# Float32 products for V, w_in split only for the last tile, and halves of 512 and 384 tokens in the second MLP

## The chip, the cores and the metric

The kernel runs on one core of a Trainium2 chip. The metric is the device time of one execution in microseconds (us), the median of several runs.

## The reference

Attention between 512 tokens and 32 state rows per head (8 batches, 8 heads of 64), in both directions, gives 544 rows of 512 features for each batch. Two MLPs follow (512 to 2048 to 512), each without a bias:

```python
a  = softmax(x @ state.T / 8);  xread = a @ state      # per batch and head
a2 = softmax(state @ x.T / 8);  sread = a2 @ x
t = concat([xread, sread])      # 4352 tokens x 512
h = t @ moe_w_in;  g = where(h >= 1, h, where(h <= -1, 0, (h + 1)**2 / 4))
t = g @ moe_w_out
h = t @ moe2_w_in;  g = max(h, 0) + alpha * min(h, 0)
out = g @ moe2_w_out
```

The weights reach the kernel as 8-byte floats, the rest of the work is done in float32.

## The kernel before, in words

**Precision.** A float32 operand can go to the matmul as it is, or it is split into a high part (a cast to float32r on ScalarE, `hi_`, line 72) and the rest (a subtraction on VectorE, `lo_`, line 75). A product of two split operands is three matmuls, hi x hi, hi x lo and lo x hi (`mm3`, line 78). The 8-byte weights are decoded by one ScalarE instruction (`dec0`) and four on VectorE (`dec1`).

**First MLP.** For the 4096 token rows of the eight batches the kernel does not form xread. It uses x_read @ w_in = a @ (state @ w_in): V = state @ w_in of a batch has 256 rows (8 heads x 32 state rows) and 2048 columns, and the hidden h is a product of the softmax weights with V (`h_mm`, line 545, tile hA). w_in is cut into four blocks of 512 columns (blk) and each into four tiles of 128 rows (c); a tile of 128 rows serves two heads. The step list (line 535) is 9 tiles of tokens (8 batches and a last tile with the 256 rows of sread) x 16 pieces of the hidden dimension. At step i the kernel issues the side work that was put at i with `at`, the products of step i + 2 into hA, the activation, the split of g of step i + 1, and the products with w_out into accA (`out_mm`, line 587). Batch 0 uses float32 products with w_out there, later ones split ones.

**V.** V of batch 0 is made by `vdirect` (line 431, tile vdp) from the split w_in and the split, block-diagonal state. V of batches 1 to 3 comes from one group of state rows, g = 0, in `vg_dir` (line 485, tile vgp): a head has 64 rows of w_in, so its matmuls use 64 of the 128 partitions, and the two heads of a tile of w_in are issued in turn into two PSUM buffers. V of batches 4 to 7 (g = 1) is made in batches 2 and 3, one head at a step, by `vg_mm` (line 496): the high and low parts of the head's 64 rows are read back from DRAM (wd) one under the other as ws, by a DMA on POOL's queue that casts (`vg_load`, line 469), and two matmuls over 128 partitions follow. ScalarE copies each result out of PSUM (vgo, line 476) and SP stores it to vd in DRAM, from where each batch loads and splits its part (vr, vw). The last tile has no V; it needs w_in itself, split, which it loads from wd (`w1s_load`, line 528).

**Around it.** PSUM has four buffers for hA, vdp, vgp and the attention's tiles (pool pp), and four for accumulators (pool pa). SBUF tiles come from two pools, 72 of 2 KB and 14 of 4 KB per partition. Most loads and stores are issued from SP in one queue; a store there waits for what it stores, and what stands behind it waits too. The attention of the next batch runs beside each batch. The order on each engine is the program's unless the compiling framework moves an instruction that is ready earlier.

**Second MLP.** Both products are done by a seven-product scheme on 2 x 2 blocks (`second`, line 929). The tokens are taken in five groups; each is two halves side by side, whose width HALF (line 37) is the column count of its matmuls. A group has 336 matmuls for the hidden layer (hB, line 771) and 336 for the output (accB, line 846), whatever the width; all weights (112 tiles of 256 KB) are loaded again for each group. Group 3 and group 4 change places in the token order (line 710).

Of the kernel before, what the change touches and what calls it, by code (L numbers as in the profile page):

```python
# [9 lines left out]
F32 = mybir.dt.float32  # L10
# [23 lines left out]
NF, NO = FF // 128, DM // 128  # L34
ROWS = S + NS
TOK = NB * ROWS
HALF = [448, 448, 448, 416, 416]


@with_exitstack  # L40
def kernel_body(ctx: ExitStack, tc: tile.TileContext, x, state, w1i, w1o, w2i, w2o, alpha, out):
# [12 lines left out]
    def V(name, dt=F32):  # L54
        return vp.tile([128, 1024], dt, tag="v", name=name)
# [4 lines left out]
    def PS(name):  # L60
        return pp.tile([128, 512], F32, tag="ps", name=name)
# [16 lines left out]
    def mm3(ps, terms):  # L78

        n = 3 * len(terms)  # L80
        k = 0
        for sh, sl, mh, ml in terms:
            for a, b in ((sh, mh), (sh, ml), (sl, mh)):
                pe.matmul(ps, a, b, start=(k == 0), stop=(k == n - 1))  # L84
                k += 1
# [5 lines left out]
    st1 = cp.tile([128, 256], F32, name="st1")  # L91


    vd = [[dp.tile([NH, 128, 512], F32, name=f"vd{g}_{k}") for k in range(4)] for g in range(2)]
    xd = dp.tile([NO, 128, TOK], F32, name="xd")
    w1d = dp.tile([8, 7, 128, 512], F32, name="w1d")
    w2d = dp.tile([8, 7, 128, 512], F32, name="w2d")
    wd = [dp.tile([2, DM, 512], F32, name=f"wd{k}") for k in range(4)]
    GRP = [1, 4]
    NR = 2  # L100

# [265 lines left out]
    def dec1(key):  # L367
        t = G.pop(("raw", key))
        r = G["dec", key]
        ri = r.bitcast(I32)  # L370
        words = t.bitcast(I32).rearrange("p (n t) -> p n t", t=2)
        lo_w, hi_w = words[:, :, 0], words[:, :, 1]
        dve.tensor_scalar(out=r, in0=r, scalar1=2.0 ** -15, scalar2=122876.0, op0=ALU.max, op1=ALU.min)
        yield
        dve.tensor_scalar(out=ri, in0=ri, scalar1=3, scalar2=0x3FFFFFFF,
                          op0=ALU.logical_shift_left, op1=ALU.bitwise_and)
        yield
        dve.scalar_tensor_tensor(out=ri, in0=lo_w, scalar=29, in1=ri,
                                 op0=ALU.logical_shift_right, op1=ALU.bitwise_or)
        yield  # L380
        dve.scalar_tensor_tensor(out=ri, in0=hi_w, scalar=-0x40000000, in1=ri,  # L381
                                 op0=ALU.bitwise_and, op1=ALU.bitwise_or)
        yield
        if key[0] == "wi":
            dec_hi(key)

    def dec_hi(key):
        name = "w_" + "_".join(map(str, key))
        h = U(name + "h", F32R)
        hi_(h, G["dec", key])  # L390
        W[key] = (h, U(name + "l", F32R))
# [5 lines left out]
    def decode(key, o):  # L397
        at(o - 1, dec0, key)
        at(o, dec1, key)
        if key[0] == "wi":  # L400
            at(o + 1, dec2, key)

    def split(t, name):
        h, l = U(name + "h", F32R), U(name + "l", F32R)
        hi_(h, t)
        lo_(l, t, h)
        return h, l

    def z_build(b):
        z = U(f"z{b}")  # L410
        pool.memset(z, 0.0)
        zz = z.rearrange("p (q r h d) -> p q r h d", q=2, r=2, h=2)
        sv = st1[:, b * 128:(b + 1) * 128].rearrange("p (q d) -> p q d", q=2)
        for k in range(4):
            p = slice(32 * k, 32 * k + 32)
            dve.tensor_copy(zz[p, :, k // 2, k % 2, :], sv[p])
        ps = PS(f"zt{b}")
        for k in range(4):
            pe.transpose(ps[:, k * 128:(k + 1) * 128], z[:, k * 128:(k + 1) * 128], ident)
        G["zf"] = U(f"zf{b}")  # L420
        act.copy(G["zf"], ps)
        G["z", b] = split(ps, f"zs{b}")

    def wi_load(blk, c):
        d_load(("wi", blk, c), w1i[c * 128:(c + 1) * 128, blk * 512:(blk + 1) * 512])

    def wi_store(blk, c):
        for k, t in enumerate(W["wi", blk, c]):
            ld.dma_start(out=wd[blk][k, c * 128:(c + 1) * 128, :], in_=t.bitcast(F32))

    def vdirect(b, blk):
        zh, zl = G["z", b]
        for q in range(2):
            ps = PS(f"vdp{b}{blk}{q}")
            mm3(ps, [(zh[:, c * 128:(c + 1) * 128], zl[:, c * 128:(c + 1) * 128], *W["wi", blk, c])
                     for c in (2 * q, 2 * q + 1)])
            h, l = U(f"vw{b}{blk}{q}h", F32R), U(f"vw{b}{blk}{q}l", F32R)
            hi_(h, ps)
            yield
            yield  # L440
            lo_(l, ps, h)
            VW[b, blk, q] = (h, l)

    def ld_stg(g):

        t = V(f"stg{g}")
        tv = t.rearrange("p (h u d) -> p h u d", h=NH, u=2)
        if g == 0:  # L450
            pool.memset(t, 0.0)
        for i in range(4):
            for u in range(2):
                hs = slice(u, NH, 2) if g == 0 else slice(0, NH)
                ld.dma_start(out=tv[32 * i:32 * i + 32, hs, u, :],
                             in_=state[GRP[g] + i, hs].rearrange("h n d -> n h d"))
        G["stg", g] = t

    def st_build(g, hh):
        t = G["stg", g]  # L460
        ps = PS(f"stp{g}{hh}")
        for k in range(4):
            c = (hh * 4 + k) * 128
            pe.transpose(ps[:, k * 128:(k + 1) * 128], t[:, c:c + 128], ident)
        ST[g, hh] = split(ps, f"sts{g}{hh}")
        if hh:
            del G["stg", g]

    def vg_load(g, blk, h):
        t = U(f"ws{g}{blk}{h}", F32R)  # L470
        pool.dma_start(out=t, in_=wd[blk][:, h * D:(h + 1) * D, :])
        G["w", g, blk, h] = t

    def vg_out(g, blk, h, ps):
        o = U(f"vgo{g}{blk}{h}")
        act.copy(o, ps)  # L476
        if g:
            G["vgo", blk, h] = o
        else:
            ld.dma_start(out=vd[g][blk][h], in_=o)  # L480

    def vg_store(blk, h):
        ld.dma_start(out=vd[1][blk][h], in_=G.pop(("vgo", blk, h)))

    def vg_dir(blk, c):
        wh, wl = W["wi", blk, c]
        ps = [PS(f"vgp0{blk}{2 * c + u}") for u in range(2)]
        for n in range(3):
            for u in range(2):
                h, rows = 2 * c + u, slice(64 * u, 64 * u + 64)  # L490
                k = slice((h % 4) * 128, (h % 4) * 128 + 128)
                pe.matmul(ps[u], ST[0, h // 4][n == 2][rows, k], (wh, wl, wh)[n][rows], start=(n == 0), stop=(n == 2))  # L492
        for u in range(2):
            vg_out(0, blk, 2 * c + u, ps[u])

    def vg_mm(g, blk, h):
        ws = G.pop(("w", g, blk, h))
        sh, sl = ST[g, h // 4]
        c = (h % 4) * 128
        ps = PS(f"vgp{g}{blk}{h}")  # L500
        pe.matmul(ps, sh[:, c:c + 128], ws, start=True, stop=False)
        pe.matmul(ps, sl[:, c:c + 128], ws, start=False, stop=True)  # L502
        vg_out(g, blk, h, ps)

    def vr_load(b, blk, q):
        g = 0 if b < 5 else 1
        i = b - GRP[g]
        t = U(f"vr{b}{blk}{q}")
        ld.dma_start(out=t, in_=vd[g][blk][4 * q:4 * q + 4, 32 * i:32 * i + 32, :])
        G["v", b, blk, q] = t  # L510
# [15 lines left out]
        return w2o[f * 128:(f + 1) * 128, :]  # L526

    def w1s_load(blk, c):
        h, l = U(f"w1s{blk}{c}h", F32R), U(f"w1s{blk}{c}l", F32R)
        for k, t in enumerate((h, l)):  # L530
            ld.dma_start(out=t.bitcast(F32), in_=wd[blk][k, c * 128:(c + 1) * 128, :])
        W["w1s", blk, c] = (h, l)


    steps = [(t, f) for t in range(NB + 1) for f in range(NF)]
# [453 lines left out]
    def at(i, fn, *a):  # L989
        side[i].append((fn, *a))  # L990
# [46 lines left out]
                at(o + 1, vr_lo, b, blk, q)  # L1037


    def vg_plan(g, start, per):  # L1040
        n = 0
        for blk in range(4):
            for h in range(NH):
                o = start + int(n * per)
                at(o - 2, vg_load, g, blk, h)
                at(o + 1, vg_mm, g, blk, h)
                at(o + 2, vg_store, blk, h)
                n += 1
        at(start - 2, ld_stg, g)
        at(start, st_build, g, 0)  # L1050
        at(start, st_build, g, 1)

    at(-2, ld_stg, 0)
    at(0, st_build, 0, 0)
    at(0, st_build, 0, 1)
    for blk in range(4):
        for c in range(4):
            at(max(1 + c, 4 * blk - 5 + c), vg_dir, blk, c)
    vg_plan(1, gi(2, 0), 1.0)

    for blk in (1, 2, 3):
        for c in range(4):
# [14 lines left out]
        at(gi(7, c + 3), xs_lo, c)  # L1077
    for blk in range(4):
        for c in range(4):
            at(gi(8, 4 * blk - 9 + c), w1s_load, blk, c)  # L1080

    def w2_plan(key, o):
        at(o - 3, d_load, key, src_w2p(*key[1:]) if key[0] == "w2i" else src_w2o(key[1]))
# [42 lines left out]
    scores(1)  # L1126
    run((dec1, ("wi", 0, 0)))
    dec0(("wi", 0, 1))
    run((first_max, 0), (first_max, 1), (dec2, ("wi", 0, 0)))
    run((first_turn, 0), (first_turn, 1), (dec1, ("wi", 0, 1)))  # L1130
    dec0(("wi", 0, 2))
    dec0(("wi", 0, 3))
    run((s6, 0, 0), (s6, 0, 1))
    dec2(("wi", 0, 1))
    run((dec1, ("wi", 0, 2)), (dec1, ("wi", 0, 3)))
    s7(0, 0)
    first_back(0)
    s7(0, 1)
    first_back(1)
    dec2(("wi", 0, 2))  # L1140
    dec2(("wi", 0, 3))
    dec0(("w1o", 0))
    run((s8, 0, 0), (s8, 0, 1), (vdirect, 0, 0))
    run((s9, 0, 0), (s9, 0, 1), (dec1, ("w1o", 0)))
# [44 lines left out]
```

## Time and profile before

| | |
|---|---|
| median of 3 runs | 1404.79 us (1403.83 to 1408.65) |
| the profiled execution | 1402.33 us, span 1400.3 us |
| first MLP, first matmul with w_out to the last hidden product of the last tile | 39.8 to 717.7 us |
| second MLP, from its first matmul | 717.7 to 1400.3 us |
| bytes moved | 312.30 MB, 223 GB/s |

The span is that of the instructions of the profiled execution; the time of a run has some 2 us around it. Engines work side by side, so a share of busy time says little of what an operation costs; that depends on which engine is waited for in the stretch in which it stands.

### The profile page before, as it was taken

The page shows a single profiled execution, that of the slowest core. Times are in us where ns is not written, and L with a number is a line of the kernel's source. Part 1 is how long each engine was busy: PE and PEld are TensorE (multiplying, and loading weights), DVE is VectorE, ACT ScalarE, POOL GpSimd, SP SyncE. Part 2 cuts the span into 40 slices and gives each one's busy share as a digit, 9 for nine tenths or more (in the row PEclk, how much of TensorE's full clock was granted, in tenths as well). Part 3 has the DMA queues.
Part 4 walks back from the last instruction along what each step waited for, and adds up shares of the span by engine and source line. Part 5 has one row for each costly group of instructions (what it writes and reads, how often), then busy time and mean ns, then how long its engine had stood idle before and what let it go on. Part 6 is the DMA issues. An engine that isn't in the chain of part 4 may idle for free.

```text
span 1400.3 us, 20902 instructions
## 1 busy us (share of the span) xinstructions
PE 1362.7 (97%) x6932; PEld 1169.8 (84%) x6932; DVE 1046.4 (75%) x1872; ACT 793.3 (57%) x1526; POOL 104.8 (7%) x123
## 2 busy tenths in 40 slices
PE   6899999999999999999999999999999999999998
PEld 4455688877788888887998999899999999999997
DVE  6877686767779787976669785778687868786873
ACT  4566676666677666775555453455454535454552
POOL 1000001231221111211101000000000000000000
PEclk9899999999999999999999999999999999999999
DMA  6897636589985665557777776777777687779774
GB/s 202 303 321 271 140 72 154 131 218 259 230 253 157 174 186 163 167 189 243 268 231 274 245 256 210 237 251 249 230 238 264 212 255 244 253 254 314 223 231 150
DMA packets 295964, 312.30 MB, mean 223 GB/s; under 512 B 144049, under 2 KB 179889, under 8 KB 295857
## 3 DMA queue, kind: packets, MB, share of 16 engines
q1 hardware_dynamic: 255504, 293.09, 66.1%
q0 software_dynamic: 33280, 8.51, 3.4%
q10 hardware_dynamic: 7072, 9.37, 1.9%
q8 instruction: 55, 0.90, 0.3%
q14 instruction: 53, 0.43, 0.1%
HBM read 237.90 MB, written 72.35 MB: 222 GB/s over the span
## 4 chain that ended last, share of the span: by engine, by line
PE 88%; DMA 5%; DVE 3%; ACT 2%; issue 1%; POOL 0%; SPq 0%; POOLq 0%; DVEq 0%; ACTq 0%
PE accB L846 24%; PE hB L771 23%; PE accA L605 20%; PE hA L84 12%; PE accA L597 4%; DMA vd<-vgo 2%; PE vgp L492 1%; PE sc L84 1%; PE vdp L84 1%; DMA ws<-wd 1%; DMA xr<-xd 1%; DMA xd<-oA 1%; PE sr L254 1%; DMA vr<-vd 0%; PE et L205 0%
## 5 line engine op out<-in xcount | busy, mean ns | idle before, releaser
L846 PE MATMUL accB<-gs,wv 128*128 128x448 f32 (+1 forms) x1680 | 336.2, 360 | 0.5 <-ACT o L864 0.5
L846 PEld LDWEIGHTS accB<-gs,wv 128*128 128x128 f32 x1680 | 315.0, 188 | 17.9 <-ACT o L864 0.8
L771 PE MATMUL hB<-xh,wu 128*128 128x448 f32 (+1 forms) x1120 | 318.9, 361 | 2.4 <-ACT p L797 1.2
L771 PEld LDWEIGHTS hB<-xh,wu 128*128 128x128 f32 x1120 | 210.1, 188 | 17.5 <-ACT p L797 2.5
L771 PE MATMUL hB<-xl,wu 128*128 128x448 f32 (+1 forms) x560 | 201.6, 360 | 0.0
L73 ACT CAST gs<-c 128x448 fp32r<-128x448 f32 (+1 forms) x200 | 109.1, 556 | 79.9 <-PE accB L846 56.7
L573 DVE SCALAR_TENSOR_TENSOR g<-y,hA 128x512 f32<-128x512 f32 (+1 forms) x144 | 93.7, 651 | 61.7 <-ACT y L571 60.1
L778 ACT ACTIVATE m<-c 128x448 f32<-128x448 f32 (+1 forms) x120 | 68.2, 568 | 119.2 <-DVE c L793 118.4
L570 ACT ACTIVATE y<-hA 128x512 f32<-128x512 f32 (+1 forms) x144 | 82.5, 573 | 73.8 <-PE hA L84 73.4
L76 DVE TENSOR_TENSOR gs<-c,gs 128x448 fp32r<-128x448 f32 (+1 forms) x200 | 114.8, 601 | 5.5 <-ACT gs L73 4.6
L780 DVE SCALAR_TENSOR_TENSOR c<-m,beta_sb,c 128x448 f32<-128x448 f32 (+1 forms) x120 | 80.8, 674 | 44.9 <-ACT m L778 42.7
L76 DVE TENSOR_TENSOR gl<-g,gh 128x512 fp32r<-128x512 f32 (+1 forms) x128 | 88.0, 688 | 33.4 <-ACT gh L73 21.7
L771 PEld LDWEIGHTS hB<-xl,wu 128*128 128x128 f32 x560 | 105.2, 188 | 5.6
L73 ACT CAST gh<-g 128x512 fp32r<-128x512 f32 (+1 forms) x128 | 75.8, 592 | 39.2 <-DVE g L573 34.6
L571 ACT ACTIVATE y<-y 128x512 f32<-128x512 f32 (+1 forms) x144 | 87.6, 608 | 3.8
L476 ACT COPY vgo<-vgp 128x512 f32<-128x512 f32 x64 | 36.4, 588 | 65.8 <-PE vgp L502 31.0
L820 DVE TENSOR_TENSOR c<-c,c 128x448 f32<-128x448 f32 (+1 forms) x120 | 71.9, 611 | 1.8
L793 DVE TENSOR_TENSOR c<-hB,u 128x448 f32<-128x448 f32 (+1 forms) x80 | 48.5, 606 | 26.1 <-PE hB L771 14.3
L597 PE MATMUL accA<-g,wf_w1o 128*128 128x512 f32 x128 | 61.5, 608 | 3.9 <-DVE wf_w1o L381 3.9
L76 DVE TENSOR_TENSOR gs<-m,gs 128x448 fp32r<-128x448 f32 (+1 forms) x80 | 46.9, 601 | 16.8 <-ACT gs L73 16.8
L73 ACT CAST gs<-m 128x448 fp32r<-128x448 f32 (+1 forms) x80 | 43.1, 556 | 25.4 <-PE accB L846 20.6
L597 PEld LDWEIGHTS accA<-g,wf_w1o 128*128 128x128 f32 x128 | 22.9, 189 | 27.5 <-issue 21.6
(951 smaller groups left out, 2695.2 us busy)
## 6 DMA issues: line engine op xcount, KB each, us to landing
wu<-w1d SPq DMA_DIRECT2D x280, 256.0 KB
wv<-w2d SPq DMA_DIRECT2D x280, 256.0 KB
vd<-vgo SPq DMA_DIRECT2D x64, 256.0 KB
vr<-vd SPq DMA_DIRECT2D x56, 256.0 KB
w1d<-wu SPq DMA_DIRECT2D x56, 256.0 KB
w2d<-wo SPq DMA_DIRECT2D x40, 256.0 KB
x<-in_x_dram SPq DMA_DIRECT2D x18, 512.0 KB
wr_wi<-in_moe_w_in_dram SPq DMA_DIRECT2D x16, 512.0 KB
```

The costliest lines, as they stand in the source:

```text
L73: act.copy(h, raw)
L76: (eng or dve).tensor_tensor(out=l, in0=raw, in1=h.bitcast(F32), op=ALU.subtract)
L84: pe.matmul(ps, a, b, start=(k == 0), stop=(k == n - 1))
L570: act.activation(out=y[:, :n], in_=ps, func=AF.Relu, bias=0.5, scale=0.5)
L571: act.activation(out=y[:, :n], in_=y[:, :n], func=AF.Square)
L573: dve.scalar_tensor_tensor(out=g[:, :n], in0=y[:, :n], scalar=1.0, in1=ps, op0=ALU.min, op1=ALU.max)
L597: pe.matmul(ACC[k], w[:, k * 128:(k + 1) * 128], g, start=(f == 0), stop=(f == NF - 1))
L605: pe.matmul(ACC[k][:, :n], a, b, start=(f == 0 and j == 0), stop=(f == NF - 1 and j == 2))
L771: pe.matmul(ps, a[:, kk], b, start=(new and m == 0), stop=(m == 5), skip_group_check=True)
L780: dve.scalar_tensor_tensor(out=g, in0=m, scalar=beta_sb[:, f:f + 1], in1=h, op0=ALU.mult, op1=ALU.add)
L820: dve.tensor_tensor(out=o, in0=x, in1=y, op=op)
L846: pe.matmul(ps, a[:, js], b, start=(new and k == 0 and n == 0), stop=(k == 7 and n == 2), skip_group_check=True)
```

## The change

w_in is no longer split when it is decoded. `vdirect` and the products for both groups use float32 operands: the decoded w_in from SBUF, which stays there until the second group is done, and the unsplit state. The second group's products move from batches 2 and 3 to batch 1, one tile of w_in (two heads) at a step, and no longer read w_in back; its group has batches 4 to 7 in rows 32 to 127 of a tile whose state batch 4 is the last one of the first group. wd keeps one float32 copy of w_in, and the last tile splits it. HALF becomes 512, 512, 384, 384, 384, whose sum is the same.

```diff
-HALF = [448, 448, 448, 416, 416]
+HALF = [512, 512, 384, 384, 384]
-    vd = [[dp.tile([NH, 128, 512], F32, name=f"vd{g}_{k}") for k in range(4)] for g in range(2)]
+    vd = [[dp.tile([NH, 128 - 32 * g, 512], F32, name=f"vd{g}_{k}") for k in range(4)] for g in range(2)]
-    wd = [dp.tile([2, DM, 512], F32, name=f"wd{k}") for k in range(4)]
+    wd = [dp.tile([DM, 512], F32, name=f"wd{k}") for k in range(4)]
...
-        if key[0] == "wi":
-            dec_hi(key)
...
-        if key[0] == "wi":
-            at(o + 1, dec2, key)
...
-        G["z", b] = split(ps, f"zs{b}")
...
     def wi_store(blk, c):
-        for k, t in enumerate(W["wi", blk, c]):
-            ld.dma_start(out=wd[blk][k, c * 128:(c + 1) * 128, :], in_=t.bitcast(F32))
+        ld.dma_start(out=wd[blk][c * 128:(c + 1) * 128, :], in_=G["dec", ("wi", blk, c)])
 
     def vdirect(b, blk):
-        zh, zl = G["z", b]
         for q in range(2):
             ps = PS(f"vdp{b}{blk}{q}")
-            mm3(ps, [(zh[:, c * 128:(c + 1) * 128], zl[:, c * 128:(c + 1) * 128], *W["wi", blk, c])
-                     for c in (2 * q, 2 * q + 1)])
+            for c in (2 * q, 2 * q + 1):
+                pe.matmul(ps, G["zf"][:, c * 128:(c + 1) * 128], G["dec", ("wi", blk, c)],
+                          start=(c == 2 * q), stop=(c > 2 * q))
...
     def ld_stg(g):
-        t = V(f"stg{g}")
-        tv = t.rearrange("p (h u d) -> p h u d", h=NH, u=2)
-        if g == 0:
-            pool.memset(t, 0.0)
+        t = U(f"stg{g}")
         for i in range(4):
-            for u in range(2):
-                hs = slice(u, NH, 2) if g == 0 else slice(0, NH)
-                ld.dma_start(out=tv[32 * i:32 * i + 32, hs, u, :],
-                             in_=state[GRP[g] + i, hs].rearrange("h n d -> n h d"))
+            ld.dma_start(out=t[32 * i:32 * i + 32].rearrange("n (h d) -> n h d", d=D),
+                         in_=state[GRP[g] + i].rearrange("h n d -> n h d"))
         G["stg", g] = t
 
+    def st_build(g):
+        t = G.pop(("stg", g))
+        ps = PS(f"stp{g}")
         for k in range(4):
+            pe.transpose(ps[:, k * 128:(k + 1) * 128], t[:, k * 128:(k + 1) * 128], ident)
+        ST[g] = U(f"sts{g}")
+        act.copy(ST[g], ps)
+
+    def vg_mm(g, blk, c):
+        w = G["dec", ("wi", blk, c)]
+        ps = [PS(f"vgp{g}{blk}{2 * c + u}") for u in range(2)]
         for u in range(2):
+            rows = slice(64 * u, 64 * u + 64)
+            pe.matmul(ps[u], ST[g][rows, c * 128:(c + 1) * 128], w[rows], start=True, stop=True)
+        for u in range(2):
+            o = G["vgo", g, blk, 2 * c + u] = U(f"vgo{g}{blk}{2 * c + u}")
+            act.copy(o, ps[u])
+
+    def vg_store(g, blk, c):
+        for h in (2 * c, 2 * c + 1):
+            ld.dma_start(out=vd[g][blk][h], in_=G.pop(("vgo", g, blk, h))[32 * g:])
...
     def w1s_load(blk, c):
+        G["w1s", blk, c] = U(f"w1s{blk}{c}")
+        ld.dma_start(out=G["w1s", blk, c], in_=wd[blk][c * 128:(c + 1) * 128, :])
+
+    def w1s_hi(blk, c):
+        h = U(f"w1s{blk}{c}h", F32R)
+        hi_(h, G["w1s", blk, c])
+        W["w1s", blk, c] = (h, U(f"w1s{blk}{c}l", F32R))
+
+    def w1s_lo(blk, c):
+        h, l = W["w1s", blk, c]
+        lo_(l, G.pop(("w1s", blk, c)), h)
...
     at(-2, ld_stg, 0)
+    at(0, st_build, 0)
+    at(gi(1, -6), ld_stg, 1)
+    at(gi(1, -2), st_build, 1)
     for blk in range(4):
         for c in range(4):
-            at(max(1 + c, 4 * blk - 5 + c), vg_dir, blk, c)
-    vg_plan(1, gi(2, 0), 1.0)
+            o = max(1 + c, 4 * blk - 5 + c)
+            at(o, vg_mm, 0, blk, c)
+            at(o, vg_store, 0, blk, c)
+            at(gi(1, 4 * blk + c), vg_mm, 1, blk, c)
+            at(gi(1, 4 * blk + c + 1), vg_store, 1, blk, c)
...
-            at(gi(8, 4 * blk - 9 + c), w1s_load, blk, c)
+            at(gi(8, 4 * blk - 10 + c), w1s_load, blk, c)
+            at(gi(8, 4 * blk - 8 + c), w1s_hi, blk, c)
+            at(gi(8, 4 * blk - 7 + c), w1s_lo, blk, c)
```

The calls of `dec2` for block 0 go from the opening sequence too.

## Rows read from the trace of the kernel before

**Rows 1.** The page's first part: busy us (share of the span) xinstructions.

```profile
PE 1362.7 (97%) x6932; PEld 1169.8 (84%) x6932; DVE 1046.4 (75%) x1872; ACT 793.3 (57%) x1526; POOL 104.8 (7%) x123
```

**Rows 2.** Busy time by stretch: us, five engines, granted clock, DMA share, GB/s.

```profile
40.00:66.00 26.00, 19.96 (x61) 11.54 (x60) 23.52 (x45) 14.23 (x26) 0.00 (x0) 0.87 0.85 278
66.00:166.00 100.00, 100.00 (x385) 53.82 (x384) 72.03 (x138) 59.42 (x109) 2.93 (x2) 1.00 0.83 257
166.00:237.30 71.30, 71.30 (x380) 58.59 (x379) 50.78 (x90) 48.51 (x91) 5.26 (x6) 1.00 0.46 111
237.30:317.30 80.00, 78.31 (x407) 63.91 (x406) 57.61 (x100) 53.93 (x101) 22.16 (x26) 1.00 0.67 176
317.30:402.90 85.60, 79.08 (x406) 63.55 (x405) 62.19 (x111) 56.18 (x108) 20.97 (x23) 1.00 0.93 247
402.90:473.50 70.60, 70.60 (x374) 57.95 (x373) 59.71 (x107) 48.56 (x89) 12.52 (x14) 1.00 0.64 188
681.70:717.70 36.00, 36.00 (x302) 36.00 (x301) 30.80 (x59) 25.31 (x65) 4.03 (x4) 1.00 0.77 262
```

**Rows 3.** The waits of PE, 0 to 717 us: us in total, times, longest.

```profile
PE accA L597 <- DVE wf_w1o L381: 3.9, 1, 3.9
...
PE vgp L501 <- DMA ws<-wd: 3.1, 1, 3.1
PE vdp L84 <- ACT w_wi_2h L73: 3.1, 1, 3.1
...
PE vgp L492 <- DVE g L573: 2.1, 1, 2.1
```

**Rows 4.** The chain that ended last, in order of time: start us, us, what.

```profile
161.31 3.43 PE accA L597 x8
...
407.13 2.72 PE accA L605 x12
...
681.89 1.44 PE accA L605 x12
...
799.73 59.52 PE accB L846 x288
...
892.56 39.18 PE hB L771 x192
...
939.03 58.37 PE accB L846 x288
...
1269.16 58.99 PE hB L771 x312
...
1334.93 58.21 PE accB L846 x309
```

**Rows 5.** The timeline of PE at 21 and 73 us: start us, us, instruction.

```profile
21.07 1.14 PE L254 MATMUL sr<-x,eh 128*32 128x64 f32 x64 [0.87 <-ACT eh L337]
...
73.56 0.40 PE L84 MATMUL hA<-ath,vw011l 128*128 128x512 f32 x1
73.89 0.50 PE L492 MATMUL vgp<-w_wi_2h,sts01h 64*128 64x512 f32 x1
...
74.78 1.98 PE L597 MATMUL accA<-g,wf_w1o 128*128 128x512 f32 x4
76.69 0.50 PE L492 MATMUL vgp<-w_wi_2h,sts01h 64*128 64x512 f32 x2
...
77.60 0.70 PE L597 MATMUL accA<-g,wf_w1o 128*128 128x512 f32 x1
```

**Rows 6.** The timeline at 34 to 49 us (three rows), and a group of the page.

```profile
34.15 8.16 SPq L455 DMA_DIRECT2D stg<-in_state_dram  x8
...
41.59 0.68 DVE L76 TENSOR_TENSOR w_wi_0l<-wf_wi,w_wi_0h 128x512 fp32r<-128x512 f32 x1
...
48.53 0.66 ACT L364 ACTIVATE wf_wi<-wr_wi 128x512 f32<-128x512 f32 x1 [5.00 <-DMA wr_wi<-in_moe_w_in_dram]
...
L476 ACT COPY vgo<-vgp 128x512 f32<-128x512 f32 x64 | 36.4, 588 | 65.8 <-PE vgp L502 31.0 <-PE vgp L492 27.4 <-DMA vd<-vgo 4.0
```

More of the change, by code (lines that the diff above doesn't have):

```diff
@@ L382, in dec1 @@
                                  op0=ALU.bitwise_and, op1=ALU.bitwise_or)
-        yield
-        if key[0] == "wi":
-            dec_hi(key)
     def dec_hi(key):
@@ L457, in ld_stg @@
         G["stg", g] = t
-    def st_build(g, hh):
-        t = G["stg", g]
-        ps = PS(f"stp{g}{hh}")
+    def st_build(g):
+        t = G.pop(("stg", g))
+        ps = PS(f"stp{g}")
         for k in range(4):
[L463 to L492, printed above, removed]
-        for u in range(2):
-            vg_out(0, blk, 2 * c + u, ps[u])
@@ L496, in vg_mm @@
[L496 to L503, printed above, removed]
+            pe.transpose(ps[:, k * 128:(k + 1) * 128], t[:, k * 128:(k + 1) * 128], ident)
[4 more added lines that the diff above has]
+        ps = [PS(f"vgp{g}{blk}{2 * c + u}") for u in range(2)]
+        for u in range(2):
+            rows = slice(64 * u, 64 * u + 64)
[3 more added lines that the diff above has]
+            act.copy(o, ps[u])
@@ L505, in vr_load @@
+    def vg_store(g, blk, c):
+        for h in (2 * c, 2 * c + 1):
+            ld.dma_start(out=vd[g][blk][h], in_=G.pop(("vgo", g, blk, h))[32 * g:])
     def vr_load(b, blk, q):
         g = 0 if b < 5 else 1
-        i = b - GRP[g]
+        i = b - (1, 5)[g]
         t = U(f"vr{b}{blk}{q}")
@@ L528, in w1s_load @@
     def w1s_load(blk, c):
[L529 to L532, printed above, removed]
+        G["w1s", blk, c] = U(f"w1s{blk}{c}")
[7 more added lines that the diff above has]
+        lo_(l, G.pop(("w1s", blk, c)), h)
     steps = [(t, f) for t in range(NB + 1) for f in range(NF)]
@@ L1037, in kernel_body @@
                 at(o + 1, vr_lo, b, blk, q)
[L1040 to L1051, printed above, removed]
     at(-2, ld_stg, 0)
-    at(0, st_build, 0, 0)
-    at(0, st_build, 0, 1)
+    at(0, st_build, 0)
+    at(gi(1, -6), ld_stg, 1)
+    at(gi(1, -2), st_build, 1)
     for blk in range(4):
         for c in range(4):
-            at(max(1 + c, 4 * blk - 5 + c), vg_dir, blk, c)
-    vg_plan(1, gi(2, 0), 1.0)
+            o = max(1 + c, 4 * blk - 5 + c)
[3 more added lines that the diff above has]
+            at(gi(1, 4 * blk + c + 1), vg_store, 1, blk, c)
     for blk in (1, 2, 3):
@@ L1128, in kernel_body @@
     dec0(("wi", 0, 1))
-    run((first_max, 0), (first_max, 1), (dec2, ("wi", 0, 0)))
+    run((first_max, 0), (first_max, 1))
     run((first_turn, 0), (first_turn, 1), (dec1, ("wi", 0, 1)))
@@ L1133, in kernel_body @@
     run((s6, 0, 0), (s6, 0, 1))
-    dec2(("wi", 0, 1))
     run((dec1, ("wi", 0, 2)), (dec1, ("wi", 0, 3)))
@@ L1139, in kernel_body @@
     first_back(1)
-    dec2(("wi", 0, 2))
-    dec2(("wi", 0, 3))
     dec0(("w1o", 0))
```

## The prediction

> **What bounds it now.** I read the page's busy shares and slices first, then the busy time of each engine by stretch, then the waits in front of TensorE, then the chain of waits for the pace of one matmul. TensorE (PE) is busy for 97% of the span, DVE (VectorE) for 75% and ACT (ScalarE) for 57% [rows 1], so the end is set by how many matmuls there are and how far apart they start. The stretches show the exceptions [rows 2]. From 40 to 66 us PE is busy for 19.96 of 26 us while DVE is busy for 23.52: there the decoding of the weights leads. Batch 1 (166.0 to 237.3) takes 71.3 us and batch 4, which has nothing of V's making in it, 70.6; batches 2 and 3, into which V of batches 4 to 7 is put, take 80.0 and 85.6, together 24.4 us more than twice 70.6, and PE is idle in 1.7 and 6.5 us of them. The waits at PE name who is late [rows 3]: the decoded w_out for 3.9 us and g for 2.1 us (both in 40 to 66), the cast of w_in for 3.1 us just before, and a reload of w_in pieces, ws, for 3.1 us in batch 3.
>
> **Prices of a matmul, from the chain** [rows 4]. A float32 matmul is recorded as two instructions: accA of batch 0 has 16 x 4 products and 128 records. Eight records take 3.43 us, 0.429 each, so a 512-column float32 product costs 0.858 us. A split (float32r) one costs 2.72/12 = 0.227 us, three of them 0.681. At 256 columns it is 1.44/12 = 0.120, at 448 columns 59.52/288 = 0.2067 in the first group of tokens, 39.18/192 = 0.2041 and 58.37/288 = 0.2027 in a later one, at 416 columns 58.99/312 = 0.1891 and 58.21/309 = 0.1884. At 2.4 GHz, the upper level, the columns alone would take 213.3, 106.7, 186.7 and 173.3 ns; what is added is 13.4, 13.3, 20.0 (down to 16.0) and 15.1 to 15.8 ns. So 512 and 256 start on at their best and 448 at its worst.
>
> By these rows a float32 product is dearer than the three split ones that it replaces, 0.858 against 0.681 us, which speaks against this change. The Trainium skill ("FP8 and Floating Point Precision", TensorE Precision Notes) says true FP32 takes four passes through the array and reduced-precision FP32 keeps fewer bits; by four passes of 0.227 a product would cost 0.908 us the V term for batch 0 below would be +3.6 instead of +2.8 us and the sum 0.6 higher.
>
> **The change, part by part.**
>
> *1. V of batch 0 (vdirect).* 48 split matmuls become 16 float32 products, 32 records: 16 x 0.858 - 48 x 0.227 = 13.7 - 10.9 = **+2.8 us** of PE work, 0.7 per block. PE is busy for all of 66 to 166 [rows 2], so three blocks, +2.1, are on the path; the first block's is in part 3.
>
> *2. V of batches 1 to 3 (vg_dir to vg_mm).* These matmuls use 64 rows of the array. One head alone holds PE from 73.89 to 74.78, 0.89 us, two heads side by side from 76.69 to 77.60, 0.91 us, and the first starts 0.33 after the matmul before it, 0.10 more than 0.227 [rows 5]. So a block costs about 1.0 us with one head or two; 0.31 of it is not matmul time but the passage to 64 rows and back. Such blocks are 19 in the trace: ten with one head, the others with 22 heads, 22.3 us in all without the 2.1 us wait, some 22 units of 1.0. In float32 a unit is 2 x 0.429 + 0.31 = 1.17 us, if two float32 heads run side by side as two split ones do. That they can is not shown for halves of the rows. It is shown for quarters of the columns: 64 records of 64 columns and 32 output columns take 1.14 us, 18 ns each [rows 5], and a 64-column float32 pass alone would take an eighth of 429, 54. All pairs: 16 x 1.17 = 18.7. All alone: 32 x 1.17 = 37.4. I take today's mixture, 21.4 units, 25 us, because what splits a pair (only one PSUM buffer of four being free) is not changed: **+2.7 us** (-3.6 to +15.1).
>
> *3. The start, to 66 us.* Removed before it: the splits of w_in (16 casts, 16 subtractions of 0.68 us [rows 6], some nine by then), of batch 0's state and of two state tiles: about 12 x 0.68 = 8 us of DVE and somewhat less of ACT. Eight state loads hold SP for 8.16 us [rows 6]; they become four, and the loads of w_in behind them, for which ACT waits 5.0 us, move up. 16 of 32 stores of 256 KB to wd go: 4.2 MB, 15 us at the 278 GB/s of that stretch. The waits of 3.9 and 2.1 us end last on DVE work that shrinks. I take them as gone, 6.0 us; the wait of 3.1 us I leave as paying for the first block in float32 (+0.7, and twice that while the clock stands at 1.2 GHz, as it does around there: 0.87 is the mean grant in 40 to 66). **-6 us** (-10 to 0: at the least the decode chain is simply late at another place).
>
> *4. V of batches 4 to 7, moved from batches 2 and 3 to batch 1.* Gone: 64 split matmuls, 14.5 us, 32 reloads on POOL's queue, the waits. Batches 2 and 3 fall to 70.6: -24.4. Batch 1 gains 16 pairs, 25 us by the mixture of part 2 (18.7 to 37.4), and of the state's eight transposes, which stand at its end, four go, 0.4 us. Four state loads instead of eight pass SP's queue six steps before it. ACT's 32 copies of 0.588 us [rows 6] move with it, 18.8 on 48.5 of then 96 us, so ACT does not bind. The stores wait on SP's queue one step after the copies and the loads of batch 2 stand behind them, as they do today in batches 2 and 3; DMA is busy for 0.46 of batch 1, so 32 x 192 KB fit. Sum: **+0.2 us** (-6 to +13).
>
> *5. w_in split for the last tile.* 16 casts and 16 subtractions come back at the end of batch 7 and in the last tile; 16 loads instead of 32 pass SP's queue, a step earlier. DVE is busy there for 30.8 of 36 us [rows 2]; some nine subtractions fall into it, 6.2 us, 37 in all, though the splits for the second MLP, which stand among them, can wait until 718. I take **+2 us** (0 to 6).
>
> *6. Halves of 512 and 384.* Each group of tokens still has 672 matmuls. Now: 672 x (0.2067 + 2 x 0.2034 + 2 x 0.18875), by the means of the paces in rows 4, 666.0 us. Then: 1344 x 0.2267 + 2016 x 0.174. No row shows 384. Bounds: 160 + 13.3 = 173.3 ns and 160 + 20 = 180; the nearest widths that carry weight are 256 and 512 (13.3, 13.4) and 416 (15.1 and more); 384 lies between 256 and 416, so 14. 304.7 + 350.8 = 655.5: **-10.5 us** (-11.9 to +1.6). The weight loads, 1169.8 us for 6932 [rows 1], 169 ns on the mean, come close to 174; but at 256 columns matmuls follow each other every 120 ns, each with its own load, so loads do not bind.
>
> Sum: 2.1 + 2.7 - 6 + 0.2 + 2 - 10.5 = **-9.5 us**. The profiled execution took 1402.33 us (span 1400.3), 2.5 under the median of the runs, 1404.79, and under all three; the sum gives 1392.8 for it and **1395.3** against the median. A measurement of this kernel tells about 0.3%, 4.2 us, from no change.
>
> **Rivals.**
>
> *A, heads always in pairs.* A float32 head has two records instead of three and batch 1 has no vdirect that wants the same four PSUM buffers. For it: where two buffers are free the two heads do go side by side, 0.91 us for both [rows 5]. Against: ten of 32 heads are alone today. Parts 2 and 4 fall by 6.3 each: 1382.7.
>
> *B, heads always alone: slower.* The two records of one product need the same rows, so the second waits for the first, and if they stand next to each other the partner cannot start beside them. Place: vg_mm. Price: 1.17 us for each of 64 heads, 75 us where I have 50: 1420. It decides from some 12 more units of the 21 possible, where the gain is used up and 0.3% lost. Against: the 18 ns of the column quarters, which are float32 too.
>
> *C, the width brings nothing.* Every matmul has the same addition whatever its width, or 384 starts on as badly as 448: part 6 is 0, 1405.8. Against: the additions of 13.3 to 20 ns in rows 4. The Trainium skill ("TensorE: Matmul & The Clock Gate", Back-to-back issue gap) gives columns / 2.4 + 2.5 ns, by which columns and count, both unchanged, would leave the time as it is. The trace has 206.7 at 448 where that gives 189.2, so the rule does not hold for this stream of loads and matmuls.
>
> *D, relief that hides.* The start keeps its waits elsewhere and the last tile pays its 6 us: 1395.3 + 6 + 4 = 1405.3.
>
> **Numbers.** Forecast 45% (its own range 1389 to 1401), A 17%, B 12%, C 14%, D 12%. Faster by over 0.3% (under 1400.6): 43 of the forecast's 45, A's 17, and 7 of C and D, 0.67. Slower: 10 of B's 12 and 3 of C and D, 0.13. Same: the rest, 0.20. Leaving out half of A below and most of B above, the range is 1380 to 1408.
>
> **What would show it.** Right: vdp records of 0.43 us, four per half; blocks of vgp with two heads of about 1.17; batches 2 and 3 at 70.6 and batch 1 near 95; no wait for wf_w1o at 43 us; 227 ns at 512 and 173 to 175 at 384 in the second MLP. Wrong: 384 at 180 or more; vgp of 0.43 one after the other, four to a pair; PE waiting for the subtraction of w1s or g in the last tile; DMA waits in the 384 groups, whose weights come each 1.04 us.

## The result, and the profile after

The changed kernel takes **1382.12 us** (median of 4 runs, 1382.02 to 1385.96) against 1404.9 for the kernel before (4 runs): ratio **0.984**, 95% interval 0.9815 to 0.9865. It is 22.8 us faster; 9.5 were forecast. The time lies in the range and the sign is right, the size is not. The profiled execution has a span of 1380.3 us, 20.0 under the 1400.3 of before; the rest of the 22.8 is that the profiled execution of before lay 2.5 under its median, as the forecast said.

The page's first part, busy us (share of the span) xinstructions, answers to [rows 1]:

```profile
PE 1353.3 (98%) x6876; PEld 1124.0 (81%) x6876; DVE 1037.1 (75%) x1867; ACT 792.0 (57%) x1523; POOL 79.4 (6%) x90
```

The busy time by stretch, with the columns of [rows 2]; from the third row on the stretches end where the first matmul of a batch starts: batches 0, 1, 2, 3, 4, and the last tile.

```profile
40.00:66.00 26.00, 21.36 (x62) 9.35 (x61) 21.18 (x43) 12.84 (x24) 0.00 (x0) 1.00 0.91 327
66.00:160.50 94.50, 93.64 (x339) 46.36 (x337) 63.11 (x123) 53.72 (x97) 2.39 (x2) 1.00 0.74 224
160.50:250.70 90.20, 90.20 (x434) 61.97 (x433) 50.23 (x89) 63.23 (x120) 2.31 (x2) 1.00 0.47 136
250.70:321.30 70.60, 70.60 (x373) 57.94 (x373) 56.44 (x101) 46.14 (x85) 10.41 (x10) 1.00 0.44 125
321.30:391.90 70.60, 70.60 (x374) 57.95 (x373) 60.59 (x110) 48.63 (x91) 10.46 (x10) 1.00 0.62 180
391.90:462.50 70.60, 70.60 (x374) 57.97 (x373) 60.12 (x107) 48.07 (x88) 11.86 (x14) 1.00 0.57 162
...
670.70:706.80 36.10, 36.10 (x302) 35.97 (x301) 33.36 (x64) 28.00 (x67) 5.62 (x4) 1.00 0.63 205
```

Batches 2 and 3 are down to 70.6, as forecast. Batch 1 takes 90.2, where the forecast had 96. From 40 to 66 us the granted clock is 1.00 where it was 0.87; what that is worth is taken up with the experiments on the start. PE waits for nothing in the last tile although DVE is now busy for 33.4 of its 36.1 us. Stage by stage, from the starts of the first matmuls in the two traces:

| stage | before | after | difference | forecast |
|---|---|---|---|---|
| start and batch 0 (parts 1 to 3) | 166.0 | 160.5 | -5.4 | -1.2 |
| batch 1 | 71.4 | 90.2 | +18.8 | +24.6 |
| batches 2 and 3 | 165.6 | 141.1 | -24.4 | -24.4 |
| batches 4 to 7 | 278.8 | 278.8 | 0.0 | 0 |
| last tile | 36.0 | 36.2 | +0.2 | +2 |
| second MLP, first to last product | 675.6 | 667.0 | -8.6 | -10.5 |
| behind it | 7.0 | 6.4 | -0.5 | 0 |

Batches 1 to 3 together are 5.6 us shorter, but not because the products of V of batches 4 to 7 became cheaper. Batches 2 and 3 were rid of 14.5 us of matmuls (64 of 0.227 us) and of 8.2 us in which PE was idle [rows 2]; batch 1 pays 18.8 us for the float32 products. The move pays because the waits go.

The waits of PE up to 717 us (us in total, times, longest) answer to [rows 3]:

```profile
...
PE accA L566 <- DVE wf_w1o L381: 3.1, 1, 3.1
PE vgp L458 <- ACT vgo L461: 2.2, 4, 0.7
PE vdp L429 <- DVE wf_wi L381: 2.2, 1, 2.2
...
```

The wait for the decoded w_out is still there, 3.1 us for 3.9; the one for g is gone; the copies out of PSUM (vgo) are new, in batch 0. The timeline of PE at 171 us, batch 1 (start us, us, instruction):

```profile
171.26 0.39 PE L84 MATMUL sc<-xh,bdl 128*128 128x512 f32 x1
171.58 1.13 PE L458 MATMUL vgp<-wf_wi,sts 64*128 64x512 f32 x4
172.64 0.50 PE L574 MATMUL accA<-gh,w_w1o_2h 128*128 128x512 f32 x1
```

The vgp row is one pair of heads: four records, two passes for each head. In the trace they start 0, 6, 533 and 540 ns after the first: the two heads run side by side. From the scores' matmul (227 ns) to accA's first the block costs 1.15 us. So it is in 14 of the 16 blocks of these products (one of them just ahead of the batch); the other two cost 1.29 and 1.66, all 16 together 19.2 us. (A block counts from its first matmul to the next matmul of another kind, plus 0.1 us for its later start.)

The chain of waits in the second MLP (start us, us, what) answers to the last four rows of [rows 4]:

```profile
796.35 65.28 PE accB L815 x288
...
1201.80 20.30 PE accB L815 x117
...
1320.10 53.57 PE accB L815 x309
```

65.28/288 is 226.7 ns at 512 columns, 20.30/117 and 53.57/309 are 173.5 and 173.4 at 384.

### The profile page after: what moved, and what is told of

The parts are those of the page before. It is cut to its first block, busy times and chain, and to the rows that moved or that the text cites. A ratio compares the mean times of both kernels' runs of the same rounds, so it can differ in the third digit from the quotient of the medians.

```text
span 1380.3 us, 20507 instructions
## 1 busy us (share of the span) xinstructions
PE 1353.3 (98%) x6876; PEld 1124.0 (81%) x6876; DVE 1037.1 (75%) x1867; ACT 792.0 (57%) x1523; POOL 79.4 (6%) x90
## 4 chain that ended last, share of the span: by engine, by line
PE 91%; DVE 4%; DMA 2%; ACT 2%; issue 1%; POOL 0%; DVEq 0%; SPq 0%; ACTq 0%
PE accB L815 24%; PE accA L574 22%; PE hB L740 22%; PE hA L84 13%; PE accA L566 4%; PE vgp L458 3%; PE sc L84 1%; DMA xr<-xd 1%; PE vdp L429 1%; PE sr L254 1%; DMA w1d<-wu 1%; PE et L205 0%; DMA wr_wi<-in_moe_w_in_dram 0%; DMA st<-in_state_dram 0%; DVE c L749 0%
## 5 line engine op out<-in xcount | busy, mean ns | idle before, releaser
L815 PE MATMUL accB<-gs,wv 128*128 128x384 f32 (+1 forms) x1680 | 332.1, 356 | 0.9 <-ACT o L833 0.9
L740 PE MATMUL hB<-xh,wu 128*128 128x384 f32 (+1 forms) x1120 | 316.0, 358 | 2.8 <-DVE m L749 1.2
L740 PE MATMUL hB<-xl,wu 128*128 128x384 f32 (+1 forms) x560 | 199.7, 357 | 0.0
L73 ACT CAST gs<-c 128x384 fp32r<-128x384 f32 (+1 forms) x200 | 109.3, 557 | 77.0 <-PE accB L815 55.8
L747 ACT ACTIVATE m<-c 128x384 f32<-128x384 f32 (+1 forms) x120 | 68.2, 568 | 118.7 <-DVE c L762 111.9
L76 DVE TENSOR_TENSOR gs<-c,gs 128x384 fp32r<-128x384 f32 (+1 forms) x200 | 114.4, 602 | 4.4 <-ACT gs L73 3.7
L749 DVE SCALAR_TENSOR_TENSOR c<-m,beta_sb,c 128x384 f32<-128x384 f32 (+1 forms) x120 | 80.9, 674 | 46.5 <-ACT m L747 44.1
L789 DVE TENSOR_TENSOR c<-c,c 128x384 f32<-128x384 f32 (+1 forms) x120 | 71.7, 607 | 1.9
L762 DVE TENSOR_TENSOR c<-hB,u 128x384 f32<-128x384 f32 (+1 forms) x80 | 48.5, 606 | 15.9 <-PE hB L740 9.2
L76 DVE TENSOR_TENSOR gs<-m,gs 128x384 fp32r<-128x384 f32 (+1 forms) x80 | 47.0, 607 | 16.5 <-ACT gs L73 16.5
```

Source lines behind the costliest of these rows:

```text
L73: act.copy(h, raw)
L76: (eng or dve).tensor_tensor(out=l, in0=raw, in1=h.bitcast(F32), op=ALU.subtract)
L740: pe.matmul(ps, a[:, kk], b, start=(new and m == 0), stop=(m == 5), skip_group_check=True)
L749: dve.scalar_tensor_tensor(out=g, in0=m, scalar=beta_sb[:, f:f + 1], in1=h, op0=ALU.mult, op1=ALU.add)
L789: dve.tensor_tensor(out=o, in0=x, in1=y, op=op)
L815: pe.matmul(ps, a[:, js], b, start=(new and k == 0 and n == 0), stop=(k == 7 and n == 2), skip_group_check=True)
```

## The experiments

Times are medians; the runs of the kernel before that were made beside them have medians of 1400.5 to 1407.7, and ratios are to those. The runs with the splits or the stores put back, with split pairs and with five widths are one execution each, so they are read by their traces.

**The two halves of the change apart.** First the kernel before with the new widths alone, then the changed kernel with the old ones.

```
-HALF = [448, 448, 448, 416, 416]
+HALF = [512, 512, 384, 384, 384]
```

> The kernel before with the second MLP's halves of 512 and 384 and nothing else. Theory (part 6 is a matter of the pace alone, and independent of the first MLP): 1344 x 0.2267 + 2016 x 0.1733 instead of 666.0 us, 11.9 less, of which the starts of the groups give some 2 to 3 us back as in the changed kernel; 8 to 10 us faster than before, about 1395.5. Rival (the two parts help each other: part of the 8.6 us that the second MLP lost comes from a last tile that brings w_in and the reloads in another order): under 6 us faster.

> The changed kernel with the halves of before (448, 448, 448, 416, 416): the change of the first MLP alone. Theory (the first MLP brings 11 us, 5.4 up to batch 1, 5.6 in batches 1 to 3, and nothing behind it): 10 to 13 us faster than before, about 1393, batch 1 at 90.2 and batches 2 and 3 at 70.6 us. Rival (parts interact): the two runs of one part each don't add up to the whole by more than 3 us.

Measured: widths alone 1398.17 (ratio 0.9939, 0.9916 to 0.9961), first MLP alone 1393.14 (0.9921, 0.9894 to 0.9949). The two savings, 0.61 and 0.79%, make 1.40%, the whole 1.6%: they add up within the intervals. In the trace of the widths alone the second MLP takes 667.0 us from first to last product, the very 667.0 of the changed kernel; in that of the first MLP alone batch 1 starts at 160.6 and takes 90.2. So each part may be judged against its own term, with one reservation: with the old widths the second MLP takes 675.6 us behind the old first MLP and 673.5 behind the new one. The last section shows the pace that differs. The widths are thus worth 8.6 us by the one trace and 6.5 by the other.

The run of the widths alone also shows one source of the scatter of the kernel before (1400.5 to 1412.0 in all its runs; the changed kernel 1382.0 to 1386.0). Its first MLP is that of before, yet batch 3 took 89.0 us here and 85.6 in [rows 2]:

```profile
317.40:406.40 89.00, 82.99 (x405) 66.50 (x405) 61.43 (x112) 56.31 (x108) 20.66 (x23) 0.94 0.89 238
...
361.00:365.00 4.00, 1.08 (x5) 0.56 (x3) 0.89 (x2) 1.53 (x3) 0.00 (x0) 0.89 0.98 304
365.00:369.00 4.00, 3.16 (x10) 2.67 (x11) 3.74 (x8) 3.96 (x9) 0.78 (x1) 0.50 0.95 273
369.00:373.00 4.00, 4.00 (x15) 3.22 (x14) 3.21 (x8) 0.47 (x1) 0.00 (x0) 0.76 0.95 291
```

In the first row, batch 3, PE idles for 6 us, hardly less than in [rows 2], but the granted clock is 0.94 on the mean where it was 1.00. The other rows are three stretches of it: PE is busy for 1.08 of 4 us, and then the clock stands at 0.50, the lower level of 1.2 GHz, and comes back. In the kernel before, PE was busy for 0.89 of the 4 us from 337 us on, and the granted clock stayed at 1.00 there; so such a gap does not always bring the clock down. Without the reloads of w_in batch 3 takes 70.6 us in every trace. Two executions do not show that this is all of the scatter.

**Heads that cannot run side by side.** The heads of V of batches 4 to 7 are regrouped so that the two adjacent ones use the same rows of the array.

```
...
-        ps = [PS(f"vgp{g}{blk}{2 * c + u}") for u in range(2)]
...
+        hs = (2 * c, 2 * c + 1) if g == 0 else (4 * (c // 2) + c % 2, 4 * (c // 2) + c % 2 + 2)
+        ps = [PS(f"vgp{g}{blk}{h}") for h in hs]
...
```

> The changed kernel with the heads of V of batches 4 to 7 regrouped: the two heads that stand next to each other use the same 64 rows of the array, so that they cannot run side by side; the number of products, copies and stores is the same. Theory (the miss is rival A: heads of different rows run side by side, 1.15 us for two, where I had counted many alone): 16 x 2 passes of 0.533 us are added, batch 1 grows from 90.2 to about 107 us, the whole is 16 to 18 us slower than the changed kernel, about 1399. Rival (the two heads only seem to run side by side and what was saved is the reloads and the waits): within 3 us of the changed kernel.

Measured: 1396.05 (1395.13 to 1398.34), some 13 to 14 us over the changed kernel. Batch 1 takes 102.1 us, 11.9 more. The timeline of PE:

```profile
174.30 0.39 PE L84 MATMUL sc<-xh,bdl 128*128 128x512 f32 x1
174.62 1.98 PE L458 MATMUL vgp<-wf_wi,sts 64*128 64x512 f32 x4
176.53 0.50 PE L574 MATMUL accA<-gh,w_w1o_2h 128*128 128x512 f32 x1
```

The same four records now start at 0, 533, 963 and 1392 ns, one after the other, and the block costs 2.00 us for 1.15. Side by side is worth 0.85 us a pair, 12.8 for the 15 pairs that lie in the batch, of which the batch shows 11.9. The expectation was too high because I gave every pass 0.533; only the first of a block takes that, the next 0.429. The rival, that only reloads and waits were saved, falls.

**Three products per head, at the same place.** In batch 1 V is made of split products again, from split pieces kept in SBUF.

```
...
-            pe.matmul(ps[u], ST[g][rows, c * 128:(c + 1) * 128], w[rows], start=True, stop=True)
...
+            for n in range(3):
+                for u in range(2):
+                    rows = slice(64 * u, 64 * u + 64)
+                    pe.matmul(ps[u], ST[2][n == 2][rows, k], (wh, wl, wh)[n][rows], start=(n == 0), stop=(n == 2))
...
```

> The kernel with the splits of w_in put back, in which V of batches 4 to 7 is now made of three split products per head again (from the split pieces in SBUF and a split state), at the same steps of batch 1; V of batches 1 to 3 stays float32. What is measured is batch 1. Theory (a head of three instructions lets other matmuls in between the heads when TensorE's queue is put in order, a head of one float32 instruction does not): in the queue four of the 16 pairs stand apart, 20 blocks instead of 16, and at 1.0 us a block (as in batch 0 of the kernel before) batch 1 takes 70.6 + 20 = 90 to 91.5 us, no less than with the dearer float32 pairs (90.2). Rival (heads run side by side in batch 1 because PSUM buffers are free there, whatever the products): 16 blocks of 1.0, 86 to 87.5 us.

Measured: batch 1 from 163.2 to 257.8, 94.6 us; the whole 1389.02 in its one run. The timeline of PE shows one of the pairs that stand apart (wx02, blocks at 175.47 and 179.53):

```profile
175.47 0.49 PE L474 MATMUL vgp<-wx02h,stsph 64*128 64x512 f32 x1
175.80 0.39 PE L474 MATMUL vgp<-wx02l,stsph 64*128 64x512 f32 x1
176.03 0.39 PE L474 MATMUL vgp<-wx02h,stspl 64*128 64x512 f32 x1
176.36 0.50 PE L590 MATMUL accA<-gh,w_w1o_2h 128*128 128x512 f32 x1
...
179.53 0.50 PE L474 MATMUL vgp<-wx02h,stsph 64*128 64x512 f32 x1
179.87 0.39 PE L474 MATMUL vgp<-wx02l,stsph 64*128 64x512 f32 x1
180.10 0.39 PE L474 MATMUL vgp<-wx02h,stspl 64*128 64x512 f32 x1
180.42 0.50 PE L590 MATMUL accA<-gl,w_w1o_2h 128*128 128x512 f32 x1
```

As expected there are 20 blocks, four pairs apart, each block near 0.99 us but one of 1.49, in all 20.4 us: more than the 19.2 of the 16 dearer float32 blocks. The batch is 3.1 us longer than 91.5; 2.2 of them are a wait of PE for g, which neither theory had, and the rest is open. The count of blocks decides between the theories: the rival's 16 are not there, although the place and the PSUM buffers are those of the changed kernel. The kernel with only the splits put back (further down), from which this one differs in the split products and the split state alone, is the control: in its trace all 16 pairs stand together and batch 1 takes 90.2 us. So the form of the products parts the heads. Whether it is the number of instructions, as the theory says, or something else in the split form, no run separates; nor does one tell why these four pairs and not the others.

**One pair per step in batch 0.** First on steps 1 to 16, then on 1 to 15, with the changed kernel beside it.

```
-            o = max(1 + c, 4 * blk - 5 + c)
+            o = 1 + 4 * blk + c
```

```
-            o = max(1 + c, 4 * blk - 5 + c)
+            o = min(4 * blk + c, 6) + 1 if blk < 2 else 4 * blk + c
```

> The changed kernel with one pair of heads of V of batches 1 to 3 per step from step 1 to 16, where the change puts up to three pairs into one step and TensorE waits for the copies out of PSUM. Theory (those waits, 2.2 us in four, and the passes apart around them are lost time on TensorE): 2 to 4 us faster than the changed kernel, about 1379, and no wait for vgo. Rival (up to 66 us the decoding on DVE and the DMA lead, so TensorE waits elsewhere): within 1 us of the changed kernel.

> The kernel of one pair per step, with the pairs of V of batches 1 to 3 on steps 1 to 15 (two on step 7) instead of 1 to 16, so that none falls into batch 1. Theory (in the run before two pairs in the first step of batch 1 cost 3.6 us for 2.3, for want of PSUM buffers): 1 to 2 us faster than that run, 3 to 4 faster than the changed kernel, about 1378.5. Rival (the wait comes back at step 7): the same as that run, 1380.8.

> The changed kernel itself, beside the run of the pairs on steps 1 to 15, on the same chip. Expected: 1382, spread under 5 us.

Measured: steps 1 to 16 1380.82 (0.9827, 0.9804 to 0.985); steps 1 to 15 1380.71 (1378.44 to 1382.64; 0.9817, 0.9789 to 0.9845); the changed kernel again 1383.21 (1382.89 to 1384.77; 0.984, 0.9813 to 0.9866). The waits of PE with steps 1 to 15, up to 300 us:

```profile
...
PE accA L566 <- DVE wf_w1o L381: 3.1, 1, 3.1
...
PE vdp L429 <- ACT vgo L461: 0.7, 1, 0.7
...
PE vgp L458 <- ACT vgo L461: 0.2, 1, 0.2
```

The waits for vgo shrink from 2.2 to 0.9 us, and batch 1 starts at 157.2 instead of 160.5 and 162.0 (160.5 is the trace that has the same granted clock as this one from 40 to 66 us, 1.00). The medians differ by 2.5 us, under the 4.2 that can be told from no change, and the intervals overlap; but no run of the new order is above the lowest of the changed kernel on that chip, and the trace shows the place. Between the two orders there is no difference in the medians; of the 1 to 2 us expected the trace has 0.2 at the end of batch 1, as the rival said. The 2 to 4 us forecast for one pair per step are not shown by the medians, and the waits for vgo did not go altogether.

**What made the start shorter.** Either the splits of w_in are computed again, unused, or its stores are issued twice.

```
...
+            hi_(h, r)
+            yield
+            lo_(l, r, h)
```

```
...
+        for d in (wd, wd2):
+            ld.dma_start(out=d[blk][c * 128:(c + 1) * 128, :], in_=G["dec", ("wi", blk, c)])
```

> The changed kernel in which each decoded tile of w_in is again cast and subtracted (16 casts on ACT, 16 subtractions on DVE), the results used by nobody; loads, stores and products stay as changed. Theory D (of the 5.4 us won up to the start of batch 1, and some 6.8 up to the scores of batch 1, most is DVE and ACT time before 66 us): batch 1 starts 3 to 7 us later than the changed kernel's 160.5 us. Rival M (it is the DMA: half of the stores of w_in and of the state's loads gone): within 1.5 us of 160.5.

> The changed kernel with the 16 stores of w_in issued twice, to two places in HBM (32 stores of 256 KB, as in the kernel before); nothing is cast more. Theory D: batch 1 starts within 1.5 us of 160.5. Rival M: 3 to 7 us later.

Measured: batch 1 starts at 163.1 with the splits and at 163.7 with the stores (1384.31 and 1385.51 in one run each). Four traces with an unchanged first MLP (two of the changed kernel, the old widths, the five widths) have 160.5 to 162.0, 161.1 on the mean. So the splits cost some 2.0 us and the stores 2.6, each beyond that spread. Against 160.5 the splits' run is 2.6 later, in neither window, and the stores' run 3.2, just inside that of M. Neither theory holds alone: the time of the splits on ACT and DVE and that of the DMA share the gain. What the state's loads add was not tried.

A third thing differs between these traces, the granted clock from 40 to 66 us, and neither theory names it. The row of the changed kernel in its second trace, with the columns of [rows 2], and below it all the traces:

```profile
40.00:66.00 26.00, 21.23 (x55) 9.73 (x56) 19.89 (x38) 11.35 (x21) 0.00 (x0) 0.87 0.81 302
```

| kernel | granted clock, 40 to 66 us | batch 1 starts at |
|---|---|---|
| changed; with the old widths | 1.00; 1.00 | 160.5; 160.6 |
| five widths | 0.93 | 161.4 |
| changed again | 0.87 | 162.0 |
| splits back; with split pairs too | 0.93; 0.93 | 163.1; 163.2 |
| stores twice | 0.93 | 163.7 |
| before; with the new widths | 0.87; 0.93 | 166.0; 165.8 |

Where the start is the changed one, its end goes along with the grant: 1.5 us of the spread. At the same grant the change wins 4.0 us (0.87) to 4.4 us (0.93) up to batch 1, so 1.0 to 1.4 of the 5.4 us in the table of stages may be the clock of these two executions. The splits cost 1.7 to 1.8 and the stores 2.4 us against the trace at 0.93, together about what the change wins there. Each of these rests on one or two traces.

**Widths that no row showed.**

```
-HALF = [512, 512, 384, 384, 384]
+HALF = [512, 512, 480, 352, 320]
...
```

The places of the last two groups in the token order (BASE) follow their new widths.

> The changed kernel with five widths in the second MLP (512, 512, 480, 352, 320; their sum is the same, so the columns of all matmuls are), to see the addition to columns / 2.4 at widths that no row shows. Theory (widths of a whole number of 128 columns start on at +13.3 ns, 256, 384 and 512 did; others later, 448 at +16 to +20, 416 at +15): 480 at 216 to 220, 352 at 162 to 167, 320 at 148 to 153 ns, the whole some 8 us slower than the changed kernel, 1390. Rival (only widths near 448 are bad): 352 at 160.0, 320 at 146.7, 480 at 213.3, the whole within 3 us of the changed kernel.

Measured: 1387.72 in its one run, span 1385.9. The chain of waits at 480, 352 and 320 columns:

```profile
1098.92 62.40 PE accB L815 x288
...
1225.98 18.73 PE accB L815 x117
...
1331.93 9.40 PE accB L815 x64
```

That is 216.7, 160.1 and 146.9 ns; the columns alone would take 200, 146.7 and 133.3 at 2.4 GHz. Neither theory holds whole: 480 is slow as the first said, 352 and 320 start on at +13.4 and +13.5 as the rival said, and the whole lies between them. The pace adds 2.3 us to the changed kernel's 654.1 (672 x (216.7 + 160.1 + 146.7) for 2016 x 173.3, beside 1344 x 226.7 in both). The stretch from the first to the last product is 5.2 us longer, 672.2 for 667.0, so 2.9 more are waits, most of them in the two narrowest groups: there single gaps between matmuls reach 1.31 us (352 columns) and 1.24 us (320).

## Why the forecast was wrong, by its steps

**The step that failed is the count of blocks in parts 2 and 4**: "I take today's mixture, 21.4 units, 25 us, because what splits a pair (only one PSUM buffer of four being free) is not changed". The price of a unit, 1.17 us, was right (1.15). The count was not: each of the two groups of 32 heads was to need 21.4 units, and batch 1 has 16 blocks. What splits a pair is the form of its products, as the run with split products beside its control shows: in four of 16 pairs of split heads other matmuls stand between the partners, with float32 heads in none. A head of three instructions gives TensorE's queue places to put something between, a float32 head, one instruction in the program, does not; that this is the reason is argued. For float32 heads missing buffers only delay the partner: in batch 0, with the same four buffers and the pairs at the same steps as before, no pair stands apart, and one whose partner gets its buffer late costs 1.6 us,

```profile
60.77 1.13 PE L458 MATMUL vgp<-wf_wi,sts 64*128 64x512 f32 x4
62.57 1.61 PE L458 MATMUL vgp<-wf_wi,sts 64*128 64x512 f32 x4 [0.67 <-ACT vgo L461]
64.11 0.70 PE L566 MATMUL accA<-g,wf_w1o 128*128 128x512 f32 x1
```

with the second head half a microsecond behind the first. (These are rows of the timeline of PE of the changed kernel at 60 us.) So rival A, at 17%, is what happened; its argument, "a float32 head has two records instead of three", was near the cause, and I had read the 19 blocks of before as a matter of buffers without looking at what stood between the heads. Their reading was off by one besides: eleven of the blocks have one head and the others 21, and their 22.3 us are some 22 units where the sum then takes 21.4; both are small beside the 5.4 units that were not there. The Trainium skill ("TensorEngine Tiling (Array Packing)", Key Properties) says that different tiles of the array load and multiply in parallel and that a change of the tiling mode drains the engine; the 1.15 against 2.00 us agree, and the 0.1 us on the first pass is in keeping with it.

Batch 1 took 5.8 us less than forecast by this. In batch 0 the blocks of V, waits included, went from 24.5 to 23.2 us where 25.0 was forecast: 1.8 more. Together 7.6 of the 10.4 us by which the sum missed the spans' difference. That rival A's 1382.7 is so near the measured time is partly luck: in batch 0 its 18.7 us were not reached, and the other terms made up for it.

**Part 1** held: vdp records follow each other every 0.43 us. **Part 3** was low by 2.4 us with the rest of batch 0: by the time of batch 1's scores the kernel is 7.7 us ahead (59.8 for 67.5), two accA records fewer. But not as told: the wait for wf_w1o stayed, and what went were small delays all along, from the splits and from the stores about equally, and 1.0 to 1.4 us of it may be the granted clock. **Part 5** was 1.8 us too dear: the split for the last tile fits beside PE. The 2 us were for a subtraction that comes too late, and none does.

**Part 6** held in its pace: 173.4 ns at 384 for the 174 taken, and 226.7 at 512. With the steady paces of the two traces (206.7, twice 202.7, twice 188.3 before; 226.7 and 173.3 after) the term is 664.4 to 654.1, -10.3, close to the -10.5 forecast. The stage shows -8.6: some 1.7 us went to waits. Those that the view names, from 717 us on, are 3.7 us in the changed kernel and 2.6 in the kernel before; of the changed kernel:

```profile
PE hB L740 <- DVE m L749: 1.2, 2, 0.6
PE hB L740 <- ACT p L766: 1.0, 1, 1.0
PE accB L815 <- ACT o L833: 0.9, 2, 0.5
...
```

In the trace matmuls stand 0.91 to 0.93 us apart near the start of each group of 384 (1031, 1157, 1275 us), and 0.80 twice between accB's; before there was one of 0.99 and one of 0.82, and the others were under 0.6. I had taken the waits as unchanged. The gaps grow further in the run with 352 and 320 columns. That a narrower group gives DVE and ACT less time for a chain of the same number of instructions is argued. The term also leans on the paces of the trace it was read from: with those of the changed kernel with the old widths (twice 202.7, 206.7, twice 186.7) it would be 662.3 to 654.1, -8.2. Rivals B and C are out: heads pair, and the widths bring 6.5 to 8.6 us by themselves. D's hidden relief did not occur.

## What to carry to other kernels

Count blocks on the array, not products: where two heads share the array by rows, a form with fewer instructions per head can win although its product is dearer (0.858 against 0.681 us here), when nothing comes between the partners: 16 float32 blocks took 19.2 us, 20 blocks of the split form 20.4. When a mixture is read from a trace, find out what makes it, in the order of the engine's queue, before carrying it over. Price a split of tokens by the measured pace of each width, in more than one trace, since 448 and 416 columns have two paces here; then add the waits at the start of each group, which grow as groups narrow. And before a stage is compared between two traces, compare the granted clock in it.

## What the hardware showed that was not expected

The addition to columns / 2.4 GHz does not grow evenly with the width: +13.3 to 13.5 ns at 256, 320, 352, 384 and 512, +16.7 at 480, +16 or +20 at 448, and +13.4 or +15 at 416. 448 has two paces in one kernel, 416 one in each of two kernels. The chain of the changed kernel with the old widths, three groups at 448 and the last at 416:

```profile
788.72 58.37 PE accB L815 x288
...
926.26 58.37 PE accB L815 x288
...
1064.00 59.52 PE accB L815 x288
...
1322.94 57.69 PE accB L815 x309
```

The first two groups go at 202.7 and the third at 206.7, where in [rows 4] the first went at 206.7 and a later one at 202.7: which one a group gets is not set by its place. The last group goes at 57.69/309 = 186.7 ns here and at 188.4 in [rows 4], with the same code of the second MLP; these paces make the 2.1 us between its two times with the old widths. What sets the pace is open. The Trainium skill ("TensorE: Matmul & The Clock Gate", Back-to-back issue gap) has one addition, 2.5 ns, for all widths, and gives it for a matmul in isolation, not for a stream of weight loads and matmuls as this one is. No width here shows it.
